# Normalizing both heads of an attention pair with one read over two PSUM banks

## The chip, the cores and the metric

The kernel runs on one core of a Trainium2 chip. The metric is device time of one execution in microseconds: 550.02 us in the median of three runs (549.77 to 550.32). The page and the trace come from one profiled execution.

## The reference, cut to what matters

```python
# attention: 2 batches, 12 heads, 448 positions, head dimension 64
scores = matmul(q, k.T) / 8
scores = where(triu, -1e9, scores); scores -= max(scores)
attn = exp(scores); attn /= sum(attn) + 1e-9
x = (attn @ v), heads side by side            # 896 tokens x 768
# first feed-forward part (768 -> 1536 -> 768)
xn = x / sqrt(mean(x*x) + 1e-6) * rms_g
x = (silu(xn @ w_gate) * (xn @ w_val)) @ w_out
# second part (768 -> 1024 -> 1024 -> 768)
x = ((x @ w1) * (x @ w2)) @ w3 @ w_out2
```

All inputs and the output are float32.

## The kernel before

**Number format.** A float32 operand is split into a float16 high part and a bfloat16 remainder (`halve`: `hi_part`, L442 to L444, and `lo_part`, L447 and L448). A product is three matmuls of such parts (L486). Weights arrive as 64-bit patterns that `fetch` (L459 to L468) turns into float32 by shifts and masks.

**Stages.** (1) Attention, in 12 pairs of heads (two batches, six pairs each). (2) Beside it, `w_prime` multiplies w3 by the last output weight, in 2 x 8 groups of 8 steps of three 384-column matmuls, on bank 3; this is work that TensorE does while attention waits. (3) `norm`, after each batch: the mean square, its power -0.5 (on GpSimd), and a matmul with the diagonal of it. (4) The gate and value stage, 12 units. Each is a product of 2 x 2 blocks in seven products instead of eight (`wino`), with sums of weight quarters (`sums`, on L482 on VectorE or L483 on GpSimd) and seven joins from PSUM (L818), 84 joins in all. (5) The output projection of the first part, (6) eight units of the second part, made as in (4), and (7) three units with the product of w3 and the output weight. From (4) on, a matmul has 448 columns.

**A pair** (`pair`): scores of both heads go to banks 0 to 2, VectorE adds the mask and takes the maximum (L556), ScalarE takes exponentials (L560). The probabilities have to be turned for the product with v. Pairs 0 to 2 turn them on TensorE (`turn`); pairs 3 to 11 split them and have a transfer turn them (`send`, L608), three a pair, queued on SyncE: two with 768 probabilities (rows of 12x128), one with 512 (8x128). The split buffers `hA` (two) and `hB` (one) are free again when the transfer has landed. Then P V: each head has four accumulation groups in its own bank, 4 or 5 (`OB`), 64 columns of output and one that holds the row sum. Three VectorE instructions a head end it: sum x 64 plus an epsilon (L657), reciprocal (L659), product into `x4` (L661). For `norm`, ScalarE sums squares of `x4` (L669).

**What sets the order.** Every instruction is given to a planner (`Plan.add`) with an engine, a cost, what it reads and writes, and a priority: a due time from the pair's or unit's number (`TP`, `GVS`, `OS`, `AS`, `FS`) and an offset by kind (`PO`). Some kinds name other engines, too (`alt`): high parts may go to VectorE or GpSimd, low parts and sums to GpSimd; `BIAS` and `THETA` say how long such work waits for its own engine. `Plan.order` plays the program forward and backward and writes each engine's list. Each engine then runs its list in that order, and waits on semaphores.

Of the kernel before, what the change touches and what calls it, by code (L numbers as in the profile page):

```python
# [8 lines left out]
F32 = mybir.dt.float32  # L9
# [6 lines left out]
ALU = mybir.AluOpType  # L16
PSUM = bass.MemoryType.PSUM

P = 128
B, H, S, D = 2, 12, 448, 64  # L20
# [6 lines left out]
NT = 4  # L27
# [3 lines left out]
GH = 2  # L31
# [4 lines left out]
SV = 2.0**6  # L36
# [1 line left out]

TP = 28.0521
WP0 = -244.6493
WPS = 48.9793
GVS = 6.4864
OS = 3.1806
AS = 4.3573
FS = -5.7914
PO = dict(dq=86.1608, dv=18.1427, vh=-4.1615, vl=31.153, sc=-23.1187, s3=-45.5392, hA=-61.1976, hl=15.902,
    hB=-24.2123, pv=19.2543, sq=-20.7221, nm=29.1952, wm=26.8125, ww=-36.4818, wx=25.6973, g=24.6307,
    a=-40.6597, o=14.4327, f=-41.7402, gm=-30.163, e=10.5623, ae=-45.2952, y=-25.9701, t1=23.8236,  # L50
    mx=19.799, dw=-6.0874)


PASSES = 8
BIAS = {"dve": 17.4016, "pool": 80.0945, "act": 139.3857}
THETA = 0.4843

DA, DB = range(3,12), range(3,12)
# [3 lines left out]
SSB, OB, GB, PB, TB = (0, 1, 2), (4, 5), (3,), (6, 7), (4, 5, 7)  # L62
# [184 lines left out]
def dve_us(n):  # L247
    return n / 960.0 + 0.07
# [26 lines left out]
def fused_kernel(ctx: ExitStack, tc, qk, v, g, wgv, wo, wab, w3t, wout, out):  # L275
    nc = tc.nc
    pl = Plan()
    add = pl.add

    const = ctx.enter_context(tc.tile_pool(name="const", bufs=1))  # L280
    psum = ctx.enter_context(tc.tile_pool(name="psum", bufs=1, space=PSUM))
    bank = [psum.tile([P, 512], F32, name=f"bank{i}") for i in range(8)]


    arena = const.tile([P, ARENA // 2], F16, name="arena")
# [58 lines left out]
    sq = [view(("sq", b), [NT, NG], F32) for b in range(B)]  # L344
    ms = [view(("ms", b), [NT], F32) for b in range(B)]
    rstd = [view(("rstd", b), [NT, 1], F32) for b in range(B)]
    mx_r = Ring("att", "mx", 3, [P, 8], F32)
    rs_r = Ring("att", "rs", 2, [P, NT, 1], F32)
    ri_r = Ring("att", "ri", 2, [P, NT, 1], F32)

    wo2 = [view(("wb", j), [NI, 384], F16 if j == 0 else BF16) for j in range(2)]
    w3 = [view(("w3", it), [2, DF2], F16) for it in range(NI)]
# [176 lines left out]
    def pair(b, gi):  # L529
        p = b * NG + gi  # L530
        x4, kx4 = x4s[:, p % 7], ("x4", p % 7)
        heads[gi] = (x4, kx4)
        t0 = p * TP
        qs, kqs = qs_r.next()
        vs, kvs = vs_r.next()
        vh, kvh = vh_r.next()
        vl, kvl = vl_r.next()
        add("sp", dma_us(P * 2 * S * 4), lambda: nc.sync.dma_start(out=qs, in_=qk[b, gi]), w=[kqs],
            prio=t0 + PO["dq"])
        add("sp", dma_us(P * 512 * 4), lambda: nc.sync.dma_start(out=vs, in_=v[b, gi]), w=[kvs],  # L540
            prio=t0 + PO["dv"])
# [8 lines left out]
        mx, kmx = mx_r.next()  # L550
# [22 lines left out]
        for i in range(3):  # L573
            w = WID[i]
# [38 lines left out]
        blk = tA.rearrange("p h c n -> p (h c) n")  # L613
        for j in range(GH if p in DA else 0):
            send(768, *hA_r.next(), pA[j][0], [pA[j][1] + (i,) for i in range(3)], blk[:, j * 12:j * 12 + 12],
                 [ktA + (c, j) for c in range(3)], 1.8, t0 + PO["hA"])
        for c in range(0, 0 if p in DA else 12, 4):
            turn([pA[j][0][:, OFF[i] + kb * P:OFF[i] + kb * P + P] for i, j, kb in order[c:c + 4]],
                 [tA[:, h, c:c + 4] for h in range(2)],
                 ktA + (c // 4,), [pA[j][1] + (i,) for i, j, _ in order[c:c + 4]], t0 + PO["hA"])  # L620
        if p in DB:
            send(512, *hB_r.next(), pB, [kpB], tB.rearrange("p h c n -> p (h c) n")[:, :, 0:P],
                 [ktB + (h,) for h in range(2)], 1.4, t0 + PO["hB"])
        else:
            turn([pB[:, kb * P:kb * P + P] for kb in range(4)], [tB[:, h, :, 0:P] for h in range(2)], ktB, [kpB], t0 + PO["hB"])

        for j in range(GH):
            ob, ko = o_b.next()
            o = ob[:, :NT * (D + 1)].rearrange("p (t c) -> p t c", t=NT)
            pr = t0 + PO["pv"] + j  # L630

            def pv(i, o=o, j=j):
                n = 3 * (i + 1)
                k = 0
                for kb in range(i + 1):
                    if i < 3:
                        c = where[i, j, kb]
                        if p in DA:
                            c = j * 12 + OFF[i] // P + kb
                        lh, ll = blk[:, c], blk[:, c + (6 if p in DA else 12)].bitcast(BF16)  # L640
                    else:
                        sl = slice(j * D, j * D + P)
                        lh, ll = tB[:, 0, kb, sl], tB[:, 1, kb, sl].bitcast(BF16)
                    r = kb * GH + j
                    for lt, rt, c in ((lh, vh[:, r], D + 1), (lh, vl[:, r], D), (ll, vh[:, r], D + 1)):
                        mm(o[:, i, :c], lt, rt, start=(k == 0), stop=(k == n - 1))
                        k += 1
            for i in range(NT):
                kt = {ktA + (where[i, j, kb] // 4,) for kb in range(i + 1)} if i < 3 else [ktB]
                kt = [k + (h,) for k in sorted(kt) for h in range(2)]  # L650
                if i < 3 and p in DA:
                    kt = [ktA + (c, j) for c in range(3)]
                add("pe", 3 * (i + 1) * 0.0286, lambda pv=pv, i=i: pv(i), r=[
                    *kt, kvh, kvl], w=[ko], prio=pr)
            rs, krs = rs_r.next()
            ri, kri = ri_r.next()
            add("dve", 0.09, lambda o=o, rs=rs: nc.vector.tensor_scalar(  # L657
                rs, o[:, :, D:D + 1], SV, 1.0e-9 * SV, op0=ALU.mult, op1=ALU.add), r=[ko], w=[krs], prio=pr)
            add("dve", 0.1, lambda rs=rs, ri=ri: nc.vector.reciprocal(ri, rs), r=[krs], w=[kri], prio=pr)  # L659
            c = j * D  # L660
            add("dve", dve_us(256), lambda o=o, ri=ri, c=c: nc.vector.tensor_tensor(  # L661
                x4[:, :, c:c + D], o[:, :, 0:D], ri.to_broadcast([P, NT, D]), op=ALU.mult),
                r=[ko, kri], w=[kx4 + (j,)], prio=pr)


        g0, m, q = SQ[b].get(gi, (0, 0, 0))
# [287 lines left out]
```

## Time and profile before

| | |
|---|---|
| median of three runs | 550.02 us |
| profiled execution, its span | 548.47 us, 546.7 us |
| TensorE busy | 524.3 us (96%) |
| VectorE busy | 495.8 us (91%) |
| ScalarE, GpSimd busy | 338.8 us (62%), 237.5 us (43%) |
| chain that ended last | TensorE 54%, VectorE 23%, transfers 8%, issue 5%, ScalarE 3% |

PE is TensorE's matmul row, PEld its weight loads, DVE VectorE, ACT ScalarE, POOL GpSimd and SP SyncE, which only issues transfers. Matmuls overlap, so a busy PE also holds time in which a matmul waits for its data; how many were done in a stretch says more. [...]

### The profile page before, as it was taken

The page shows a single profiled execution, that of the slowest core. Times are in us where ns is not written, and L with a number is a line of the kernel's source. Part 1 is how long each engine was busy: PE and PEld are TensorE (multiplying, and loading weights), DVE is VectorE, ACT ScalarE, POOL GpSimd, SP SyncE. Part 2 cuts the span into 40 slices and gives each one's busy share as a digit, 9 for nine tenths or more (in the row PEclk, how much of TensorE's full clock was granted, in tenths as well). Part 3 has the DMA queues.
Part 4 walks back from the last instruction along what each step waited for, and adds up shares of the span by engine and source line. Part 5 has one row for each costly group of instructions (what it writes and reads, how often), then busy time and mean ns, then how long its engine had stood idle before and what let it go on. Part 6 is the DMA issues. An engine that isn't in the chain of part 4 may idle for free.

```text
span 546.7 us, 9215 instructions
## 1 busy us (share of the span) xinstructions
PE 524.3 (96%) x3442; PEld 286.6 (52%) x3442; DVE 495.8 (91%) x909; ACT 338.8 (62%) x492; POOL 237.5 (43%) x198
## 2 busy tenths in 40 slices
PE   6899999999899999999999999999999999999997
PEld 4565565564666554444555455555555555454553
DVE  6999999989959999999999999899658999999953
ACT  5988887896678676557464767676336553633210
POOL 4534364676453837053656420140211846673400
PEclk9999999999999999999999999999999999999999
DMA  8888799999951133334242446517104211000021
GB/s 276 288 278 263 222 252 218 258 248 184 279 112 59 34 127 130 122 109 173 70 162 78 158 172 252 208 59 236 52 0 168 65 59 59 0 1 0 35 101 68
DMA packets 55197, 77.02 MB, mean 141 GB/s; under 512 B 39792, under 2 KB 41328, under 8 KB 55152
## 3 DMA queue, kind: packets, MB, share of 16 engines
q1 hardware_dynamic: 55152, 76.43, 48.1%
q8 instruction: 27, 0.44, 0.3%
q14 instruction: 18, 0.15, 0.1%
HBM read 64.23 MB, written 2.75 MB: 123 GB/s over the span
## 4 chain that ended last, share of the span: by engine, by line
PE 54%; DVE 23%; DMA 8%; issue 5%; ACT 3%; POOL 0%; DVEq 0%; SPq 0%; ACTq 0%
PE bank L486 54%; DVE arena L818 6%; DVE arena L447 6%; DMA arena<-arena 5%; DVE cv L468 3%; DVE st L482 3%; DVE cv L461 2%; DVE arena L482 2%; DMA st<-in_wout 2%; ACT st L464 1%; DMA st<-in_w3t 1%; DVE arena L556 1%; ACT arena L442 1%; ACT arena L560 1%; DVE arena L547 0%
## 5 line engine op out<-in xcount | busy, mean ns | idle before, releaser
L486 PE MATMUL bank<-arena 128*128 128x448 f16 (+10 forms) x2976 | 446.1, 315 | 14.7 <-ACT wpr L516 3.9
L486 PEld LDWEIGHTS <-arena 128*128 128x128 f16 x3048 | 248.8, 98 | 229.0 <-issue 22.1
L464 ACT ACTIVATE st<-st 128x768 uint16<-128x768 uint16 (+2 forms) x72 | 117.6, 1658 | 32.6 <-DVE cv L461 29.9
L818 DVE TENSOR_TENSOR arena<-bank,arena 128x448 f32<-128x448 f32 x161 | 92.1, 612 | 18.1 <-PE bank L486 17.8
L442 ACT ACTIVATE arena<-arena 128x448 f16<-128x448 f32 (+2 forms) x90 | 53.9, 612 | 40.4 <-DVE arena L482 27.8
L468 DVE SCALAR_TENSOR_TENSOR cv<-st,cv 128x768 int32<-128x768 int32 (+2 forms) x84 | 75.1, 903 | 2.8 <-ACT st L464 2.6
L448 POOL TENSOR_TENSOR arena<-arena 128x448 bf16<-128x448 f32 (+2 forms) x29 | 49.6, 1713 | 56.7 <-ACT arena L442 44.5
L486 PE MATMUL bank<-xs,arena 128*128 128x448 f16 x360 | 72.4, 353 | 1.7 <-ACT arena L815 1.1
L447 DVE TENSOR_TENSOR arena<-arena 128x448 bf16<-128x448 f32 (+2 forms) x80 | 61.2, 780 | 2.4 <-ACT arena L442 1.1
L442 ACT ACTIVATE arena<-cv 128x768 f16<-128x768 f32 (+2 forms) x61 | 41.0, 679 | 32.5 <-DVE cv L468 18.6
L461 DVE TENSOR_SCALAR cv<-st 128x768 int32<-128x768 int32 (+2 forms) x84 | 50.0, 600 | 7.3 <-DMA st<-in_wout 4.2
L448 POOL TENSOR_TENSOR arena<-cv,arena 128x384 bf16<-128x384 f32 (+2 forms) x31 | 44.4, 1434 | 24.8 <-ACT arena L442 24.2
L483 POOL TENSOR_TENSOR arena<-arena 128x448 f32<-128x448 f32 x23 | 30.1, 1314 | 35.6 <-DVE arena L818 21.3
L560 ACT ACTIVATE arena<-arena 128x384 f32<-128x384 f32 (+3 forms) x84 | 41.2, 518 | 5.8 <-DVE arena L556 5.2
L444 POOL TENSOR_SCALAR arena<-cv 128x384 f16<-128x384 f32 (+2 forms) x22 | 20.2, 918 | 55.7 <-DVE cv L468 31.1
L447 DVE TENSOR_TENSOR arena<-cv,arena 128x768 bf16<-128x768 f32 (+2 forms) x53 | 43.3, 824 | 0.8 <-POOL arena L444 0.7
L447 DVE TENSOR_TENSOR arena<-st,arena 128x1536 bf16<-128x1536 f32 (+1 forms) x25 | 42.1, 1682 | 0.1
L482 DVE TENSOR_TENSOR arena<-arena 128x448 f32<-128x448 f32 x57 | 37.5, 668 | 4.1 <-ACT arena L864 4.1
L442 ACT ACTIVATE arena<-st 128x1536 f16<-128x1536 f32 (+1 forms) x22 | 30.5, 1389 | 17.4 <-DVE st L482 7.7
L556 DVE CUSTOM_DVE_ANT_0 arena<-bank,arena 128x384 f32<-128x384 f32 (+3 forms) x84 | 35.7, 441 | 1.9 <-PE bank L486 1.2
L486 PEld LDWEIGHTS bank<-arena 64*128 64x128 f32 (+2 forms) x288 | 27.5, 178 | 19.0 <-issue 5.2
L815 ACT ACTIVATE arena<-bank 128x448 f32<-128x448 f32 x23 | 12.6, 546 | 25.3 <-PE bank L486 15.2
(69 smaller groups left out, 310.2 us busy)
## 6 DMA issues: line engine op xcount, KB each, us to landing
st<-in_wgv SPq DMA_DIRECT2D x24, 768.0 KB, 4.5
st<-in_wab SPq DMA_DIRECT2D x16, 768.0 KB, 4.4
st<-in_wo SPq DMA_DIRECT2D x12, 768.0 KB, 4.4
st<-in_w3t SPq DMA_DIRECT2D x16, 512.0 KB, 4.8
st<-in_wout SPq DMA_DIRECT2D x16, 384.0 KB, 3.9
arena<-in_qk SPq DMA_DIRECT2D x12, 448.0 KB, 5.1
arena<-in_v SPq DMA_DIRECT2D x12, 256.0 KB, 3.8
out_t<-arena SPq DMA_DIRECT2D x12, 224.0 KB, 1.9
```

Source lines behind the costliest of these rows:

```text
L442: add("act", act_us(n), lambda: nc.scalar.activation(hi, src, AF.Copy), r=r, w=w, prio=prio, alt=(("dve", dve2_us(n), lambda: nc.vector.te ...
L447: add("dve", dve_us(n), lambda: nc.vector.tensor_tensor(lo, src, hi, op=ALU.subtract), r=r, w=w, prio=prio, port=True, alt=(("pool", pool_ ...
L448: port=True, alt=(("pool", pool_us(n), lambda: nc.gpsimd.tensor_tensor(lo, src, hi, op=ALU.subtract)),))
L461: add("dve", dve2_us(n), lambda: nc.vector.tensor_scalar(cv, hi, 3, 0x3FFFFFFF, op0=ALU.logical_shift_left, op1=ALU.bitwise_and), r=[ks], ...
L464: add("act", ACT_TOP * n - 0.08, lambda: nc.scalar.activation(b[:, :, 2], b[:, :, 1], AF.Copy, scale=1.0 / 8192, bias=-8191.0 / 16384), w= ...
L468: add("dve", dve_us(n), lambda: nc.vector.scalar_tensor_tensor(cv, hi, -0x3FFFFFF9, cv, op0=ALU.bitwise_and, op1=ALU.bitwise_or), r=[ks], ...
L482: add("dve", dve_us(n), lambda: nc.vector.tensor_tensor(out, a, b, op=op), port=True, alt=(("pool", pool_us(n) + 0.1, lambda: nc.gpsimd.te ...
L483: ("pool", pool_us(n) + 0.1, lambda: nc.gpsimd.tensor_tensor(out, a, b, op=op)),), **kw)
L486: nc.tensor.matmul(*a, **k)
L556: add("dve", dve_us(w), lambda: nc.vector.tensor_tensor_reduce(out=sc[:, :w], in0=ss[:, :w], in1=m, scale=-CSC, scalar=3.0e38, op0=ALU.add ...
L560: add("act", act_us(w) + 0.1, lambda: nc.scalar.activation(dst, sc[:, :w], AF.Exp, bias=mx[:, c:c + 1], scale=-1.0), r=[ksc, kmx + (c,)], ...
L818: add("dve", dve_us(S), lambda: nc.vector.tensor_tensor(dst, ps, y, op=ALU.add), r=[kp, ky], w=[kd], prio=p)
```

## The change

`o_b` still hands out banks 4 and 5, head 0 and head 1, but both are now views of one PSUM tile of two banks. The three normalizing instructions move out of the loop over heads: one set per pair reads both banks, and it waits for both heads' products. The planner's cost of a turning transfer goes from 1.8 to 1.9 and from 1.4 to 1.8. All due times, offsets and the three `BIAS` values have new numbers, of which two lines are shown.

```diff
-PO = dict(dq=86.1608, dv=18.1427, vh=-4.1615, vl=31.153, sc=-23.1187, s3=-45.5392, hA=-61.1976, hl=15.902,
...
+PO = dict(dq=77.7592, dv=-40.5165, vh=-6.106, vl=33.6109, sc=-35.4643, s3=-35.7215, hA=-116.2841,
...
-BIAS = {"dve": 17.4016, "pool": 80.0945, "act": 139.3857}
+BIAS = {"dve": 23.0593, "pool": 108.7578, "act": 107.956}
...
-    bank = [psum.tile([P, 512], F32, name=f"bank{i}") for i in range(8)]
+    two = psum.tile([P, GH, 512], F32, name="banks45")
+    bank = [two[:, i - 4] if i in OB else psum.tile([P, 512], F32, name=f"bank{i}") for i in range(8)]
...
-                 [ktA + (c, j) for c in range(3)], 1.8, t0 + PO["hA"])
+                 [ktA + (c, j) for c in range(3)], 1.9, t0 + PO["hA"])
...
-                 [ktB + (h,) for h in range(2)], 1.4, t0 + PO["hB"])
+                 [ktB + (h,) for h in range(2)], 1.8, t0 + PO["hB"])
...
-            rs, krs = rs_r.next()
-            ri, kri = ri_r.next()
-            add("dve", 0.09, lambda o=o, rs=rs: nc.vector.tensor_scalar(
-                rs, o[:, :, D:D + 1], SV, 1.0e-9 * SV, op0=ALU.mult, op1=ALU.add), r=[ko], w=[krs], prio=pr)
-            add("dve", 0.1, lambda rs=rs, ri=ri: nc.vector.reciprocal(ri, rs), r=[krs], w=[kri], prio=pr)
-            c = j * D
-            add("dve", dve_us(256), lambda o=o, ri=ri, c=c: nc.vector.tensor_tensor(
-                x4[:, :, c:c + D], o[:, :, 0:D], ri.to_broadcast([P, NT, D]), op=ALU.mult),
-                r=[ko, kri], w=[kx4 + (j,)], prio=pr)
+        o = two[:, :, :NT * (D + 1)].rearrange("p j (t c) -> p j t c", t=NT)
+        kos = [("bank", i) for i in OB]
+        rs, krs = rs_r.next()
+        ri, kri = ri_r.next()
+        pr = t0 + PO["pv"] + 1
+        four = lambda t: t.rearrange("p (j t) c -> p j t c", j=GH)
+        add("dve", 0.09, lambda: nc.vector.tensor_scalar(
+            four(rs), o[:, :, :, D:D + 1], SV, 1.0e-9 * SV, op0=ALU.mult, op1=ALU.add), r=kos, w=[krs], prio=pr)
+        add("dve", 0.1, lambda: nc.vector.reciprocal(ri, rs), r=[krs], w=[kri], prio=pr)
+        add("dve", dve_us(512), lambda: nc.vector.tensor_tensor(
+            x4.rearrange("p t (j c) -> p j t c", j=GH), o[:, :, :, 0:D], four(ri).to_broadcast([P, GH, NT, D]),
+            op=ALU.mult), r=[*kos, kri], w=[kx4 + (j,) for j in range(GH)], prio=pr)
```

Line numbers of the changed kernel are one higher from L283 on and four higher behind the normalization (L657, L659, L661 become L662, L664, L665).

VectorE's list where the last pair is normalized, before (`cv` and `st` are buffers in which gate weights are unpacked; banks 65 and 66 are banks 4 and 5):

```order
L468 SCALAR_TENSOR_TENSOR cv_78<-st_74,cv_78 128x768
L657 TENSOR_SCALAR arena<-bank_65 128x4
L468 SCALAR_TENSOR_TENSOR cv_77<-st_73,cv_77 128x768
L657 TENSOR_SCALAR arena<-bank_66 128x4
L659 RECIPROCAL arena<-arena 128x4 x2
L661 TENSOR_TENSOR arena<-bank_65,arena 128x4x64
L661 TENSOR_TENSOR arena<-bank_66,arena 128x4x64
L676 TENSOR_REDUCE arena<-arena 128x4
```

The same place in VectorE's list now, from the normalization of the last pair but one on:

```order
L662 TENSOR_SCALAR arena<-banks_61 128x8
L548 SCALAR_TENSOR_TENSOR arena<-arena 128x512
L664 RECIPROCAL arena<-arena 128x8
L462 TENSOR_SCALAR cv_77<-st_73 128x768
L665 TENSOR_TENSOR arena<-banks_61,arena 128x2x4x64
L469 SCALAR_TENSOR_TENSOR cv_77<-st_73,cv_77 128x768
L662 TENSOR_SCALAR arena<-banks_61 128x8
L664 RECIPROCAL arena<-arena 128x8
L665 TENSOR_TENSOR arena<-banks_61,arena 128x2x4x64
L462 TENSOR_SCALAR cv_76<-st_72 128x768
L467 TENSOR_SCALAR st_72<-st_72 128x768
```

Six instructions of the pair became three over both banks, and unpacking moved behind them, ahead of the mean square.

SyncE's list at the last turning transfers, before (the three of the last pair are the last three):

```order
L608 DMA_TRANSPOSE arena<-arena 128x12x128
L540 DMA arena<-in_v 128x512
L459 DMA st_72<-in_wgv 128x1536
L608 DMA_TRANSPOSE arena<-arena 128x12x128
L459 DMA st_73<-in_wgv 128x1536
L608 DMA_TRANSPOSE arena<-arena 128x8x128
L608 DMA_TRANSPOSE arena<-arena 128x12x128
```

The same place in SyncE's list now:

```order
L609 DMA_TRANSPOSE arena<-arena 128x12x128
L541 DMA arena<-in_v 128x512
L609 DMA_TRANSPOSE arena<-arena 128x12x128
L609 DMA_TRANSPOSE arena<-arena 128x8x128
L609 DMA_TRANSPOSE arena<-arena 128x12x128
L460 DMA st_72<-in_wgv 128x1536
L460 DMA st_71<-in_wgv 128x1536
```

Two loads of gate weights (`wgv`) moved behind the last turn.

GpSimd's list at its end, before (`wpr` is the product of `w_prime`; its quarters' sums have 256 elements):

```order
L483 TENSOR_TENSOR st_72<-wpr,st_72 128x256
L483 TENSOR_TENSOR st_73<-wpr 128x256
L483 TENSOR_TENSOR st_72<-wpr 128x256
L483 TENSOR_TENSOR st_71<-st_71,wpr 128x256
L448 TENSOR_TENSOR arena<-wpr,arena 128x768
L483 TENSOR_TENSOR st_72<-wpr 128x256
L483 TENSOR_TENSOR st_71<-wpr,st_71 128x256
L483 TENSOR_TENSOR st_72<-wpr,st_72 128x256
```

GpSimd's list at its end now:

```order
L484 TENSOR_TENSOR st_72<-wpr 128x256
L484 TENSOR_TENSOR arena<-arena 128x448
L449 TENSOR_TENSOR arena<-st_71,arena 128x1024
L445 TENSOR_SCALAR arena<-st_70 128x1024
L449 TENSOR_TENSOR arena<-wpr,arena 128x768
```

Most of these sums went to VectorE's list.

## Rows read from the trace of the kernel before

**Rows 1.** Stretches by stage: length, then busy time (instructions) of each engine, clock, transfers.

```profile
0.00:70.00 70.00, 61.75 (x469) 37.88 (x470) 62.06 (x164) 56.92 (x87) 29.70 (x43) 1.00 0.83 268
70.00:100.00 30.00, 28.39 (x343) 16.29 (x342) 28.45 (x93) 25.03 (x55) 18.11 (x20) 1.00 1.12 238
100.00:153.50 53.50, 49.78 (x553) 31.45 (x552) 49.42 (x128) 41.71 (x79) 32.53 (x27) 1.00 1.12 232
153.50:168.70 15.20, 14.59 (x139) 11.38 (x140) 9.21 (x18) 11.59 (x27) 5.63 (x6) 1.00 0.29 76
168.70:310.50 141.80, 137.97 (x725) 70.23 (x724) 140.37 (x201) 90.82 (x113) 74.02 (x52) 1.00 0.32 109
310.50:404.00 93.50, 93.50 (x495) 48.37 (x496) 82.40 (x124) 57.82 (x69) 19.25 (x12) 1.00 0.45 156
404.00:505.60 101.60, 100.91 (x533) 51.88 (x532) 98.71 (x145) 48.56 (x60) 52.17 (x34) 1.00 0.14 47
505.60:546.70 41.10, 37.38 (x197) 19.12 (x196) 25.20 (x42) 6.37 (x8) 6.12 (x5) 1.00 0.18 68
```

**Rows 2.** The chain that ended last, pieces in order: start, length, what.

```profile
146.64 6.85 DMA arena<-arena
153.53 5.37 PE bank L486 x66
...
310.48 151.33 PE bank L486 x799
```

**Rows 3.** Groups by form, VectorE: busy us, mean ns, idle time ahead and its releasers.

```profile
L447 DVE TENSOR_TENSOR arena<-arena 128x448 bf16<-128x448 f32 x60 | 39.7, 680 | 0.5 <-POOL arena L444 0.5
L482 DVE TENSOR_TENSOR arena<-arena 128x448 f32<-128x448 f32 x57 | 37.5, 668 | 4.1 <-ACT arena L864 4.1
L447 DVE TENSOR_TENSOR arena<-st,arena 128x1536 bf16<-128x1536 f32 x19 | 34.8, 1831 | 0.1
...
L661 DVE TENSOR_TENSOR arena<-bank,arena 128x256 f32<-128x256 f32 x24 | 9.5, 411 | 0.0
...
L482 DVE TENSOR_TENSOR st<-cv 128x384 f32<-128x384 f32 x13 | 8.5, 656 | 0.0
...
L466 DVE TENSOR_SCALAR st<-st 128x768 uint16<-128x768 uint16 x8 | 8.5, 1061 | 0.0
...
L601 DVE TENSOR_TENSOR arena<-bank,arena 128x512 bf16<-128x512 f32 x12 | 8.1, 678 | 0.1
...
L482 DVE TENSOR_TENSOR st<-wpr 128x256 f32<-128x256 f32 x7 | 4.1, 588 | 0.0
...
L659 DVE RECIPROCAL arena<-arena 128x4 f32<-128x4 f32 x24 | 3.9, 168 | 0.0
...
L657 DVE TENSOR_SCALAR arena<-bank 128x4 f32<-128x4 f32 x24 | 3.5, 151 | 1.2 <-PE bank L486 1.2
```

**Rows 4.** VectorE in order of time, normalizing instructions back to back: start, us, instruction.

```profile
129.02 0.15 DVE L657 TENSOR_SCALAR arena<-bank 128x4 f32<-128x4 f32 x1
129.09 0.41 DVE L661 TENSOR_TENSOR arena<-bank,arena 128x256 f32<-128x256 f32 x1
129.42 0.16 DVE L659 RECIPROCAL arena<-arena 128x4 f32<-128x4 f32 x1
129.50 0.59 DVE L556 CUSTOM_DVE_ANT_0 arena<-bank,arena 128x448 f32<-128x448 f32 x1
```

**Rows 5.** Line L482 alone: shortest, median and longest in ns, first and last start.

```profile
L482 DVE TENSOR_TENSOR arena<-arena x57: 606/611/1550, 166.7 to 504.4; 128x448 f32<-128x448 f32 x57
```

**Rows 6.** SyncE's queue in order of time, the last pair's turning transfers.

```profile
141.70 0.38 SPq L459 DMA_DIRECT2D st<-in_wgv  x1
142.27 2.72 SPq L608 DMA_TRANSPOSE arena<-arena  x1
146.21 0.33 SPq L459 DMA_DIRECT2D st<-in_wgv  x1
146.64 6.20 SPq L608 DMA_TRANSPOSE arena<-arena  x2
```

**Rows 7.** Who waited for whom: TensorE for the normalizing product, us in total, times, longest.

```profile
PE bank L486 <- DVE arena L661: 1.4, 2, 1.2
```

More of the change, by code (lines that the diff above doesn't have):

```diff
@@ L37 @@
 CSC = 1.0 / 8.0
[L41 to L47, printed above, removed]
-PO = dict(dq=86.1608, dv=18.1427, vh=-4.1615, vl=31.153, sc=-23.1187, s3=-45.5392, hA=-61.1976, hl=15.902,
-    hB=-24.2123, pv=19.2543, sq=-20.7221, nm=29.1952, wm=26.8125, ww=-36.4818, wx=25.6973, g=24.6307,
-    a=-40.6597, o=14.4327, f=-41.7402, gm=-30.163, e=10.5623, ae=-45.2952, y=-25.9701, t1=23.8236,
-    mx=19.799, dw=-6.0874)
+TP = 27.8378
+WP0 = -245.8258
+WPS = 50.5471
+GVS = 6.7175
+OS = 3.5723
+AS = 4.4797
+FS = -8.2001
+PO = dict(dq=77.7592, dv=-40.5165, vh=-6.106, vl=33.6109, sc=-35.4643, s3=-35.7215, hA=-116.2841,
+    hl=22.6624, hB=-33.9427, pv=24.7154, sq=-60.5725, nm=29.7288, wm=27.3571, ww=-34.6109, wx=54.8086,
+    g=20.3381, a=-40.8814, o=-2.6777, f=-32.9588, gm=-31.3816, e=28.8562, ae=-39.8349, y=-19.4493,
+    t1=22.8432, mx=18.7762, dw=-21.4831)
 PASSES = 8
-BIAS = {"dve": 17.4016, "pool": 80.0945, "act": 139.3857}
+BIAS = {"dve": 23.0593, "pool": 108.7578, "act": 107.956}
 THETA = 0.4843
@@ L347, in fused_kernel @@
     mx_r = Ring("att", "mx", 3, [P, 8], F32)
-    rs_r = Ring("att", "rs", 2, [P, NT, 1], F32)
-    ri_r = Ring("att", "ri", 2, [P, NT, 1], F32)
+    rs_r = Ring("att", "rs", 2, [P, GH * NT, 1], F32)
+    ri_r = Ring("att", "ri", 2, [P, GH * NT, 1], F32)
     wo2 = [view(("wb", j), [NI, 384], F16 if j == 0 else BF16) for j in range(2)]
```

## Prediction

> **What bounds the kernel now.** I read the table of stages first, then the chain of waits, then VectorE's rows, and the issue queue last. The stages [rows 1] fall into two kinds. From 168.7 us on (the four feed-forward stages) TensorE does little but multiply: the longest unbroken stretch of the chain holds 799 matmuls in 151.33 us, 0.1894 us each [rows 2]. At that rate the 725 matmuls of 168.7 to 310.5 need 137.3 of 141.8 us, so 4.5 us are waits; the 495 of 310.5 to 404 and the 533 of 404 to 505.6 need 93.8 and 100.9 us, so waits there are under 1 us. All that can be won after 168.7 us is then some 5 us. VectorE is busy for 140.37 of 141.8 us in the first of these stages: the 4.5 us are waits for VectorE. In 404 to 505.6 it is busy for 98.71 of 101.6 us and only just keeps up.
>
> Before 168.7 us TensorE is not the bound. VectorE is busy for 62.06 of the first 70 us, with the transfers at a share of 0.83, then for 28.45 of 30 and 49.42 of 53.5 us. In 153.5 to 168.7 it is busy for only 9.21 of 15.2 us, since it waits for the last pair of heads. The chain there runs through the turning transfers: one of 6.85 us on it lands at 153.49, and the last P V products start on it [rows 2]. So the end of the attention is set by the last pair's splits on VectorE, its turning transfers, and then the normalization this change edits.
>
> **The change part by part.** The sums are made against the profiled execution, 548.47 us (span 546.7 and 1.77 around it); the median of the runs is 550.02, 1.55 above it, and I add that at the end.
>
> *Normalization.* Per head there are three VectorE instructions: 0.151, 0.168 and 0.411 us long [rows 3]. On a busy VectorE they cost less than they last, because the next one starts before the one ahead has ended: 129.02 to 129.09, 129.09 to 129.42, 129.42 to 129.50 [rows 4], so 0.07, 0.33 and 0.08, with rounding 0.49 per head and 0.98 per pair. Now there are three per pair. The two short ones keep their price, 0.15 together; the product grows from 256 to 512 elements, and the nearest pair of rows that read PSUM puts 256 more elements at 0.678 - 0.411 = 0.267 us [rows 3], so 0.60. A pair costs 0.75, a saving of 0.23, and 12 pairs save 2.8 us. If the two-bank read cost nothing extra per element it would be 0.50 per pair, 5.8 us; if it took twice the 256-element product and its own start, nothing is saved beyond the short pair, 1.8 us. I take 2.8.
>
> [...] The spacing of the rows [rows 4] shows that most of the short instructions' length is covered here.
>
> *Work that changes engine.* The planner picks an engine for each split and each sum of the weights. Of the 104 sums of weight quarters, 61 stood on VectorE and 82 do now. I count VectorE's rows up to the last of the 84 joins of the gate and value stage, apart from the normalization: 12 more sums of 384 (0.656), 4 fewer products or sums of 448 (0.668), 4 fewer low parts of 448 (0.680) and 2 fewer of 1536 (1.831) [rows 3]: +7.9 - 2.7 - 2.7 - 3.7 = -1.2. The single rows left over are some 14, near zero. With the normalization VectorE has 4.0 us less to do by then. Where it falls: about 2 us before the last split of the last pair (10 of the 12 normalizations, the rest cancels), about 2 between there and the first join, none inside the stage.
>
> Behind that join VectorE has 8 more sums of 256 (0.588), 5 more low parts of 448, 3 more products of 448, 3 fewer shifts of 768 (1.061), and small ones worth -1.8: +4.7 + 3.4 + 2.0 - 3.2 - 1.8 = +5.1 us. GpSimd is relieved of the same work. That gives some back: a sum of 448 on VectorE takes 0.606 at the least, 0.611 in the median, and up to 1.550 [rows 5], and its mean in the table is 0.668 [rows 3], a tenth more than undisturbed. Less GpSimd work means fewer such stretched rows.
>
> *Turning transfers.* Their number and size stay. In the queue the load of gate weights between the last pair's turns (146.21 [rows 6]) now stands behind them, and of seven such loads ahead of the last turn five are left. These loads share the transfer engines, whose share is 1.12 from 70 to 153.5 us [rows 1]. I price this at nothing, with up to 3 us below as its bound: two loads less in a stretch of 53.5 us whose last hop is 6.85 us.
>
> *The sum.* Attention: VectorE is busy for 93% of 70 to 153.5 us, so most of its 2.0 us comes through: -1.7 (bounds 0, if the turns alone set the pace, and -4.6 with the transfers relieved as well). The hand-over and gate stage: -1.8 of the 2.0 us, for VectorE has hardly an idle microsecond there and TensorE has 4.5 us of waits to give back (bounds 0 and -4.0). Behind 404 us: 5.1 us more in a stretch where VectorE has 2.9 idle, less what GpSimd's relief gives back: +1.0 (bounds 0 and +4). Together -2.5: 546.0 for a profiled execution, **547.5** as a median.
>
> **The rivals.**
> *The shared banks become a wait (slower).* Before, head 0's bank was free as soon as that head was normalized; now both wait for head 1's products, and the next pair's first product waits for the joint instruction. TensorE takes its list in order, so scores, w' steps and products behind it stand too. Today two such waits cost 1.4 us [rows 7]. There are 11 hand-overs. From the last product of a pair, the joint work needs 0.75 us plus what stands between its three rows, mostly two score reductions, some 2 us in all; in TensorE's list the tightest hand-over (pair 9 to 10) has one score pair and four w' steps ahead, 12 matmuls at about 0.16 (an estimate, 0.1894 x 384/448), 1.9 us plus the scores. It decides if VectorE stands more than a microsecond behind at most hand-overs: then 11 x 0.7 = 8 us, half of it hidden where the turns are late anyway, +4, less the 2 that the gate stage gains: 552. Against it: the planner knows the dependency and spread the products out, and VectorE's list is shorter. [...]
> *The turns set the end anyway (no change).* The last hop of 6.85 us [rows 2] does not care for 2 us of VectorE, which then idles longer than today's 6 us before 168.7; the gate stage's gain pays for the end: 549.5.
> *The end pays it all back.* VectorE's 5.1 us behind the gate stage come through by 3 to 4 where it is already at 98.71 of 101.6: 550 to 551.
> *The transfers are relieved too (faster still).* The attention ends 4.6 earlier: 544.5.
>
> **How the numbers follow.** What a measurement tells from no change is about 0.2%, 1.1 us. The forecast has 0.45 (0.39 of it faster, 0.06 within), faster still 0.16, turns set the end 0.16 (all within), paid back 0.10 (half within, half slower), shared banks 0.13 (slower). Faster 0.55, within 0.27, slower 0.18. The range leaves out the last tenth on either side: 543.5 to 552.
>
> **What would show it.** Right: the first 448-column product starts 1 to 4 us before 168.7; the three joint rows are spaced by 0.75 in all, the product lasts near 0.68; VectorE's wait for P V products stays near 1.2 us [rows 3] and TensorE's for the joint product at or below 1.4 us; the 4.5 us of waits up to the end of the gate stage shrink by about 2; VectorE is busier than 98.71 in the second unit stage. Wrong: the first product starts later than 168.7, TensorE's waits for the joint product are above 4 us, or the waits behind 404 us grow by more than 2 us.

## The result, and the profile after

The changed kernel takes 557.81 us in the median of four runs (556.89 to 558.93), against 550.14 for the kernel before beside it: a ratio of 1.0141, 95% interval 1.0118 to 1.0164. The forecast was 547.5 with a range of 543.5 to 552. It was wrong in size and in sign. The profiled execution has a span of 555.1 us.

The stretches of [rows 1], of the changed kernel:

```profile
0.00:70.00 70.00, 62.26 (x477) 38.27 (x477) 61.10 (x151) 54.63 (x85) 38.25 (x52) 0.95 0.79 264
...
153.50:168.70 15.20, 12.06 (x119) 9.31 (x118) 9.21 (x14) 7.64 (x22) 3.98 (x4) 0.89 0.44 159
168.70:310.50 141.80, 135.49 (x724) 70.88 (x723) 137.86 (x195) 89.82 (x114) 80.42 (x51) 1.00 0.31 106
310.50:404.00 93.50, 92.17 (x487) 47.51 (x486) 84.45 (x129) 64.17 (x69) 15.25 (x9) 1.00 0.46 161
404.00:505.60 101.60, 100.85 (x534) 52.05 (x532) 96.41 (x147) 48.75 (x62) 39.71 (x27) 1.00 0.15 47
```

The windows are those of the kernel before; from the gate stage on, the changed kernel is 2.6 us and more behind it in them. The first row has a clock of 0.95 and GpSimd at 38.25 us, where it was 1.00 and 29.70. In 153.5 to 168.7 TensorE is busy for 12.06 us instead of 14.59, at a clock of 0.89. In the gate and value stage VectorE is no longer busy nearly throughout (137.86 for 140.37): it has idle time that it had not before, while GpSimd does more (80.42 for 74.02). In 310.5 to 404, where TensorE had not idled, it now does 487 matmuls for 495.

VectorE's groups by form, which answer to [rows 3]:

```profile
L483 DVE TENSOR_TENSOR arena<-arena 128x448 f32<-128x448 f32 x56 | 34.1, 630 | 4.3 <-ACT arena L704 2.5 <-ACT arena L868 1.3 <-ACT arena L843 0.5
...
L665 DVE TENSOR_TENSOR arena<-banks,arena 128x512 f32<-128x512 f32 x12 | 8.2, 682 | 0.0
...
L664 DVE RECIPROCAL arena<-arena 128x8 f32<-128x8 f32 x12 | 2.3, 194 | 0.1
L662 DVE TENSOR_SCALAR arena<-banks 128x8 f32<-128x8 f32 x12 | 1.9, 156 | 1.9 <-PE banks L487 1.9
```

The joint product takes 0.682 us, next to the 0.68 that was reckoned. From the start of each normalizing row to the next row's start, idle time left out, a pair costs 0.86 us in the mean of the twelve, where the trace before has 1.04: 2.2 us saved in all, and 2.8 were reckoned.

TensorE from 168 us on, in order of time: the waits of over 0.3 us ahead of matmuls that write the two-bank tile (`banks`), with the idle time and its releaser in brackets.

```profile
169.40 2.00 PE L487 MATMUL banks<-arena 128*128 128x128 f32 x16 [0.36 <-ACT arena L704]
...
214.43 1.86 PE L487 MATMUL banks<-arena 128*128 128x448 f16 x9 [0.87 <-DVE arena L822]
...
255.60 1.86 PE L487 MATMUL banks<-arena 128*128 128x448 f16 x9 [0.92 <-DVE arena L822]
...
353.51 3.56 PE L487 MATMUL banks<-arena 128*128 128x448 f16 x18 [0.69 <-ACT arena L868]
...
401.98 3.56 PE L487 MATMUL banks<-arena 128*128 128x448 f16 x18 [0.63 <-ACT arena L868]
...
545.56 0.73 PE L487 MATMUL banks<-arena 128*128 128x448 f16 x3 [0.63 <-ACT arena L819]
```

These are six waits, 4.1 us. In the program's semaphores the reason can be counted: 19 instructions of TensorE on bank 4 or 5 wait for a reader of the other bank, and at least 15 readers on VectorE and ScalarE wait for a product in the other one. In the kernel before there is none of either. The program orders a tile as a whole: banks 4 and 5 serve the mean square and all later products as well, and there they are now one buffer.

The end of the attention, VectorE, GpSimd and TensorE in that order:

```profile
156.00 0.17 DVE L662 TENSOR_SCALAR arena<-banks 128x8 f32<-128x8 f32 x1 [1.32 <-PE banks L487]
156.20 0.20 DVE L664 RECIPROCAL arena<-arena 128x8 f32<-128x8 f32 x1
156.44 0.69 DVE L665 TENSOR_TENSOR arena<-banks,arena 128x512 f32<-128x512 f32 x1
...
159.94 0.17 DVE L683 TENSOR_SCALAR arena<-arena 128x4 f32<-128x4 f32 x1
...
163.25 1.32 DVE L688 TENSOR_TENSOR arena<-arena 128x512 f32<-128x512 f32 x1 [1.87 <-POOL arena L685]
```

```profile
159.97 1.00 POOL L484 TENSOR_TENSOR st<-cv 128x384 f32<-128x384 f32 x1 [14.34 <-DVE arena L680]
161.04 1.19 POOL L484 TENSOR_TENSOR st<-st,cv 128x384 f32<-128x384 f32 x1
162.19 1.02 POOL L685 TENSOR_TENSOR arena<-arena,mhalf 128x4 f32<-128x4 f32 x1
```

```profile
164.62 3.53 PE L487 MATMUL banks<-arena 128*128 128x128 f32 x16 [2.56 <-DVE arena L688]
...
171.24 1.86 PE L487 MATMUL bank<-xs,arena 128*128 128x448 f16 x9
```

The last joint product ends at 157.13. Before, the last two products ended at 157.53:

```profile
156.78 0.75 DVE L661 TENSOR_TENSOR arena<-bank,arena 128x256 f32<-128x256 f32 x2
```

Then the mean square's power (L685) stands behind two sums in GpSimd's list and starts 2.1 us after its input is there. TensorE idles for 2.56 us, and its next 16 matmuls take 3.53 us, at a granted clock of 0.52 (165 to 168 us, below). The first 448-column product starts at 171.24 instead of 168.67.

A table from the traces, one profiled execution each (us), for this kernel and most of the experiments told below. First and last product are the starts of the first and last matmul of 448 columns from the gate stage on.

| kernel | first product | last product | between |
|---|---|---|---|
| before | 168.67 | 542.63 | 373.96 |
| changed | 171.24 | 551.04 | 379.80 |
| before, one tile | 171.91 | 549.17 | 377.26 |
| two tiles | 169.39 | 543.48 | 374.09 |
| banks apart behind | 172.78 | 547.90 | 375.12 |
| changed, filled | 170.07 | 549.86 | 379.79 |
| apart, filled | 172.52 | 547.32 | 374.80 |
| two tiles, filled | 169.76 | 544.52 | 374.76 |
| power first | 167.53 | 543.07 | 375.54 |

The changed kernel loses 5.8 us between the two and 2.6 ahead of the first. A single execution can lie far from its kernel's median: that of the two tiles is the fastest of six (549.32, median 552.51), and that of "apart, filled" is 2.7 us slower than its median.

### The profile page after: what moved, and what is told of

Its sections match the earlier page's. It is cut to its first block, busy times and chain, and to the rows that moved or that the text cites. A ratio compares the mean times of both kernels' runs of the same rounds, so it can differ in the third digit from the quotient of the medians.

```text
span 555.1 us, 9164 instructions
## 1 busy us (share of the span) xinstructions
PE 525.2 (95%) x3434; PEld 288.4 (52%) x3434; DVE 499.4 (90%) x885; ACT 341.4 (61%) x493; POOL 223.6 (40%) x185
## 5 line engine op out<-in xcount | busy, mean ns | idle before, releaser
L487 PE MATMUL bank<-arena 128*128 128x448 f16 (+7 forms) x1802 | 345.4, 359 | 12.8 <-DVE arena L822 5.1
L487 PE MATMUL banks<-arena 128*128 128x65 f16 (+4 forms) x1174 | 114.9, 254 | 8.9 <-DVE arena L688 2.6
L449 POOL TENSOR_TENSOR arena<-cv,arena 128x384 bf16<-128x384 f32 (+2 forms) x36 | 57.6, 1604 | 62.2 <-ACT arena L443 50.2
L822 DVE TENSOR_TENSOR arena<-bank,arena 128x448 f32<-128x448 f32 x127 | 73.8, 612 | 6.9 <-PE bank L487 6.5
L487 PE MATMUL bank<-xs,arena 128*128 128x448 f16 (+1 forms) x252 | 50.8, 352 | 0.0
L449 POOL TENSOR_TENSOR arena<-arena 128x448 bf16<-128x448 f32 (+2 forms) x29 | 40.0, 1388 | 22.2 <-ACT arena L443 17.1
L561 ACT ACTIVATE arena<-arena 128x128 f32<-128x128 f32 (+3 forms) x84 | 41.0, 518 | 9.2 <-DVE arena L557 5.1
L557 DVE CUSTOM_DVE_ANT_0 arena<-bank,arena 128x256 f32<-128x256 f32 (+3 forms) x84 | 35.2, 440 | 4.9 <-ACT arena L561 2.5
L448 DVE TENSOR_TENSOR arena<-cv,arena 128x768 bf16<-128x768 f32 (+2 forms) x48 | 38.0, 799 | 0.0
L822 DVE TENSOR_TENSOR arena<-banks,arena 128x448 f32<-128x448 f32 x34 | 20.4, 613 | 12.2 <-PE banks L487 12.2
```

The costliest lines, as they stand in the source:

```text
L448: add("dve", dve_us(n), lambda: nc.vector.tensor_tensor(lo, src, hi, op=ALU.subtract), r=r, w=w, prio=prio, port=True, alt=(("pool", pool_ ...
L449: port=True, alt=(("pool", pool_us(n), lambda: nc.gpsimd.tensor_tensor(lo, src, hi, op=ALU.subtract)),))
L487: nc.tensor.matmul(*a, **k)
L557: add("dve", dve_us(w), lambda: nc.vector.tensor_tensor_reduce(out=sc[:, :w], in0=ss[:, :w], in1=m, scale=-CSC, scalar=3.0e38, op0=ALU.add ...
L561: add("act", act_us(w) + 0.1, lambda: nc.scalar.activation(dst, sc[:, :w], AF.Exp, bias=mx[:, c:c + 1], scale=-1.0), r=[ksc, kmx + (c,)], ...
L822: add("dve", dve_us(S), lambda: nc.vector.tensor_tensor(dst, ps, y, op=ALU.add), r=[kp, ky], w=[kd], prio=p)
```

## The experiments

**Two separate tiles.** The changed kernel's lists word for word; sums and products read bank by bank, each pair of reads in the joint one's place.

```diff
-    two = psum.tile([P, GH, 512], F32, name="banks45")
-    bank = [two[:, i - 4] if i in OB else psum.tile([P, 512], F32, name=f"bank{i}") for i in range(8)]
+    bank = [psum.tile([P, 512], F32, name=f"bank{i}") for i in range(8)]
```

> The changed kernel with banks 4 and 5 as two PSUM tiles again. The lists of all engines stay word for word; VectorE reads the two banks in two instructions each for the sums and the products (12 x about 0.4 us = 4.8 us more VectorE time, nothing else). Theory A (a tile of two banks is tracked as one, so that a product in bank 4 waits for the reader of bank 5 and the other way round): the waits of TensorE behind its first 448-column product, 11.5 us in the changed kernel and 6.5 before, fall to 7 or less; time 551.5 to 554. Theory B (the refitted numbers give worse lists): nothing changes there, and VectorE's extra work comes on top: 557.5 to 561.

Measured: 552.51 us (549.32 to 556.74, six runs), ratio 1.0085 [1.0048, 1.0123], in theory A's range. The six waits listed above are gone, and the length between first and last product is that of before.

**The kernel before with the joint tile alone.** The opposite edit: six instructions a pair as before, lists word for word.

```diff
-    bank = [psum.tile([P, 512], F32, name=f"bank{i}") for i in range(8)]
+    two = psum.tile([P, GH, 512], F32, name="banks45")
+    bank = [two[:, i - 4] if i in OB else psum.tile([P, 512], F32, name=f"bank{i}") for i in range(8)]
```

> The kernel before with banks 4 and 5 as one PSUM tile of two banks and nothing else: same lists, normalization still per head. Theory A: waits between the two banks, in the attention (the products of head 1 wait while head 0 is normalized) and in every later stage: 554 to 564. Theory B: no change, 549 to 551.

Measured: 556.55 us (555.04 to 558.75), 1.0148 [1.0113, 1.0182], in theory A's range. Declaring the two banks as one tile, with nothing else changed, costs as much as the whole change. TensorE's waits ahead of `banks` include these:

```profile
347.38 3.57 PE L487 MATMUL banks<-arena 128*128 128x448 f16 x18 [0.63 <-ACT arena L865]
483.87 3.56 PE L487 MATMUL banks<-arena 128*128 128x448 f16 x18 [1.37 <-DVE arena L819]
543.68 0.73 PE L487 MATMUL banks<-arena 128*128 128x448 f16 x3 [0.63 <-ACT arena L816]
```

Here the hand-overs inside the attention cost something, too. The first product comes 3.2 us later than before, and TensorE's waits for normalizing instructions (in total, times, longest) come to 2.7 us where it waited 1.4 before [rows 7]:

```profile
PE banks L487 <- DVE arena L662: 2.0, 4, 0.8
PE banks L487 <- DVE arena L658: 0.7, 3, 0.3
```

In this kernel one head's products wait while the other head is normalized; in the changed kernel both are normalized at once.

**The two halves of the change, planned anew.** The numbers and turning costs without the joint normalization, then the joint normalization with the old numbers and costs.

> The kernel before with the changed kernel's numbers (due times, offsets, biases, cost of a turning transfer), normalization per head, two tiles. Theory A: most of the loss is gone, 549 to 553. Theory B: the numbers carry the loss, 555 to 559.

> The changed kernel with the numbers of the kernel before: joint read over one tile of two banks, old due times, offsets, biases and transfer costs. Theory A: 554 to 559, with the waits behind the first 448-column product at 10 us or more. Theory B: 548 to 551.

Measured: 572.24 us, 1.0424 [1.0382, 1.0466], and 569.79 us, 1.0387 [1.0361, 1.0413]. Both missed every theory. Two more kernels took the turning costs alone: the kernel before with the new ones, the changed kernel with the old ones.

> The kernel before, with nothing changed but the two turning costs (1.8 to 1.9 and 1.4 to 1.8), so the lists are planned anew with the old numbers. If the numbers are fitted to one set of lists and any other input gives lists that nobody has selected, 555 to 575, like the two halves of the change (572 and 570). If the half's slowness came from the normalization's form alone, 548 to 552.

> The changed kernel with the two turning costs as before, the new numbers and the joint normalization kept. If the numbers are fitted to one set of lists, 562 to 575; if the turning costs matter little to the lists, 556 to 560.

Measured, two runs each: 562.22 us, 1.0224 [1.0189, 1.0260], and 569.43 us, 1.0356 [1.0322, 1.0390]. In all four, most of the loss lies between first and last product: 388 to 403 us in their profiled executions, instead of 374. In the first and the last of the four, TensorE also has its longest waits around the end of the attention, of 3.2, 5.2 and 10.1 us (total, times, longest):

```profile
PE bank L486 <- ACT wpr L516: 9.6, 7, 3.2
PE bank L486 <- DVE arena L684: 5.6, 2, 5.2
```

```profile
PE banks L487 <- DVE arena L688: 11.0, 2, 10.1
```

The planner's numbers fit the lists they were chosen for. All four other inputs gave lists 2 to 4% slower, so the price of one half can't be had by leaving the other out. The experiments below keep the planned lists, but for the instructions that they add or replace and for one place in the order of two of them.

**Banks apart behind the attention.** The joint normalization stays; when the last pair is normalized, the two-bank tile is given back and two separate ones take its place.

```diff
+    def apart():
+        early.__exit__(None, None, None)
+        pool = ctx.enter_context(tc.tile_pool(name="apart", bufs=1, space=PSUM))
+        for i in OB:
+            late[i] = pool.tile([P, 512], F32, name=f"bank{i}")
...
+            if p == B * NG - 1:
+                apart()
```

> The changed kernel's lists word for word and its joint normalization, but banks 4 and 5 are one tile only until the last pair is normalized, and two separate tiles from there on. Theory A (the time is lost where a product or join on one of the two banks waits for the other bank's reader, in the mean square's matmuls and the feed-forward stages): 551.5 to 553.5, as with two separate tiles throughout (552.5); TensorE's waits for the joins of L822 fall from 6.9 us to 3 or 4. Rival B (the pair's hand-over inside the attention carries it): 556 to 558, no change from the changed kernel. Rival C (the granted clock carries it): 556 to 558 too, with the clock still at 0.985 to 0.993.

Measured: 553.52 us (550.03 to 555.12, eleven runs), 1.0067 [1.0041, 1.0094]: by the ratios 0.74%, some 4.1 us, less than the changed kernel. TensorE's waits for the joins fall from 6.9 to 4.0 us. So these 4 us are not lost in the hand-overs inside the attention, which still go through one tile.

**The gaps filled.** `filler` issues two matmuls on zeros: 13 times ahead of the third turn on TensorE, 10 times ahead of the last mean square's first matmul.

```diff
+                for _ in range(13 if turns[0] == 3 else 0):
+                    filler()
...
+                for _ in range(10 if first else 0):
+                    filler()
```

> The changed kernel with 26 matmuls on zeros of 252 columns ahead of the third turn on TensorE (16.4 to 19.7 us, where it idles 3.3 us) and 20 ahead of the first matmul of the last mean square (162 to 164.6 us, where it idles 2.6 us), all else alike. The two stretches behind these gaps ran at 0.64 and 0.51 (20 to 28 us) and at 0.52 (165 to 168 us). Theory C (the lost clock carries the time): 551 to 553, mean clock 0.997 or more. Theory A: the clock rises to 0.997, but attention is not bound by TensorE before 160 us, and only the 1.5 us at 165 to 168 come back: 555.5 to 557.

> Both edits: banks apart behind the attention, and the two gaps filled. If A and C act side by side, the gains add up: 552.5 for the first less 1.5 to 2 for the second, 550.5 to 551. If the clock carries most, 547 to 549. If B holds, 555 or more.

> Two separate tiles throughout (sums and products read bank by bank, five VectorE instructions a pair in the joint ones' places) and the two gaps filled. Against the kernel with the banks apart behind the attention and the gaps filled, this one has 24 more VectorE instructions of 0.07 to 0.33 us spacing, 2 to 3 us in all. If VectorE's time in the attention comes through, as the prediction held, it is 1.5 to 2.5 us slower than that one; if not, the same within 1 us. Its own time by A and C: 550.5 to 552; against two tiles without filling (552.5) the filling is worth 1 to 3 us.

Measured: 555.81 us (553.74 to 556.93), 1.0119 [1.0084, 1.0154]; with the banks apart 550.50 (547.59 to 554.28, twelve runs), 1.0017 [0.9989, 1.0044]; with two tiles 550.33 (548.44 to 551.76, twelve runs), 1.0015 [0.9995, 1.0036]. Stretches around the two gaps, the changed kernel and then the same filled; the third number from the end is the granted clock:

```profile
16.00:20.00 4.00, 0.70 (x7) 0.33 (x4) 4.00 (x9) 3.12 (x6) 2.18 (x3) 1.00 0.90 312
20.00:24.00 4.00, 4.00 (x34) 2.76 (x34) 3.64 (x10) 3.27 (x6) 2.85 (x3) 0.64 0.86 259
24.00:28.00 4.00, 4.00 (x50) 3.04 (x48) 3.70 (x10) 4.00 (x7) 2.19 (x4) 0.51 0.84 304
162.00:165.00 3.00, 0.44 (x3) 0.38 (x2) 1.75 (x3) 2.27 (x3) 2.03 (x3) 0.91 0.00 0
165.00:168.00 3.00, 3.00 (x17) 3.00 (x16) 1.37 (x3) 0.00 (x0) 0.00 (x0) 0.52 0.00 0
```

```profile
20.00:24.00 4.00, 3.75 (x42) 2.68 (x41) 4.00 (x12) 4.00 (x7) 2.04 (x3) 1.00 0.80 256
24.00:28.00 4.00, 3.99 (x57) 2.49 (x58) 2.86 (x9) 3.22 (x6) 3.02 (x4) 1.00 0.91 309
162.00:165.00 3.00, 2.57 (x24) 1.99 (x22) 1.39 (x2) 2.27 (x3) 2.39 (x3) 1.00 0.00 0
165.00:168.00 3.00, 2.88 (x24) 2.74 (x24) 2.05 (x4) 0.98 (x2) 0.00 (x0) 1.00 0.02 5
```

Behind a stretch with TensorE busy for 0.70 of 4 us the clock is 0.64 and then 0.51, and from 28 to 32 us it is 1.00 again; behind one with 0.44 of 3 us it is 0.52. With the gaps filled it is 1.00 from 20 to 28 us and from 162 to 168. Over the runs, the mean clock is 0.990 for the changed kernel and 0.996 filled. By the ratios, the filling is worth 0.22% (1.2 us) by itself, and there the intervals overlap, 0.50% (2.7 us) with the banks apart and 0.70% (3.8 us) with two tiles. In the changed kernel that is what theory A expected and not theory C: the first product comes 1.2 us earlier, and the length behind it stays at 379.8. The last two kernels differ by 0.2 us: reading both banks at once, 36 instructions instead of 60, brings nothing that can be measured here. What it saves and what its hand-overs through one tile may cost inside the attention are not told apart.

**The power first.** In the kernel with two tiles filled, the two sums ahead of the power on GpSimd move behind it (and 16 of the 20 matmuls on zeros at that place go).

```diff
+    at = next(k for k, f in enumerate(issue) if f is power[1])
+    held = [k for k, f in enumerate(issue[:at]) if any(f is q for q in pool_sums)][-2:]
+    issue = [f for k, f in enumerate(issue[:at + 1]) if k not in held] + [issue[k] for k in held] + issue[at + 1:]
```

> Two separate tiles and the filled start, as in the kernel with two tiles filled (550.3), and on GpSimd the power of the last mean square moved ahead of two sums of 384 that stand before it in the changed kernel's list (with only 4 matmuls on zeros left ahead of the mean square's first matmul). In that kernel the power starts 2.1 us after VectorE has its input, because the two sums run first (160.58 to 162.82). Theory T (the end of the attention is a chain: last turn, normalization, squares, power, diagonal, matmuls): the first 448-column product starts 1.5 to 2.2 us earlier, 548.2 to 549. Rival (VectorE's splits behind the matmuls are late anyway, so the chain has slack): within 0.5 us of 550.3.

Measured: 549.38 us (547.91 to 551.33, twelve runs) beside 550.00 for the kernel before, 0.9987 [0.9969, 1.0005]. That lies between the ranges of the two theories. The power now starts at 160.18, 0.1 us after its input, and the first product at 167.53, 2.2 us earlier than in the kernel with two tiles filled; 0.6 us of these stood ahead of the power already, since the last normalizing product ends at 157.30 instead of 157.90:

```profile
160.18 1.26 POOL L699 TENSOR_TENSOR arena<-arena,mhalf 128x4 f32<-128x4 f32 x1 [14.73 <-DVE arena L697]
```

```profile
167.53 1.86 PE L492 MATMUL bank<-xs,arena 128*128 128x448 f16 x9
```

Of the 2.2 us some 1.5 are left in the time (0.28% by the two ratios, whose intervals overlap): the chain is there in the trace, as expected, and part is given back in the gate and value stage (134.3 us, and 133.4 with two tiles filled, from the first product to the end of the 725th matmul of 448 columns, counted here and in the last experiment from the program's start with the attention's own). This is the best of the kernels that compute everything, and it can't be told from the kernel before.

**Products made twice.** The kernel before, each normalizing product issued a second time.

```diff
+            def twice(o=o, ri=ri, c=c):
+                for _ in range(2):
+                    nc.vector.tensor_tensor(x4[:, :, c:c + D], o[:, :, 0:D], ri.to_broadcast([P, NT, D]), op=ALU.mult)
+            add("dve", dve_us(256), twice, r=[ko, kri], w=[kx4 + (j,)], prio=pr)
```

> The kernel before, lists word for word, with each of the 24 normalizing products on VectorE made twice, the second over the first. That is 24 x 0.33 = 7.9 us more for VectorE, all but 0.7 of it ahead of the last pair's end. The prediction's step (VectorE is busy for 93% of 70 to 153.5 us, so most of what it is relieved of, or loaded with, comes through): +5 to +7, 554.5 to 557. Theory T (the turning transfers and hand-overs pace the pairs, VectorE's small work lies in its waits): +0 to +2.5, 549.5 to 552.

Measured: 555.91 us (554.40 to 557.53), 1.0111 [1.0090, 1.0132], +5.9.

VectorE's group of these products, and two of them in order of time:

```profile
L664 DVE TENSOR_TENSOR arena<-bank,arena 128x256 f32<-128x256 f32 x48 | 19.7, 418 | 0.8
```

```profile
155.45 0.87 DVE L664 TENSOR_TENSOR arena<-bank,arena 128x256 f32<-128x256 f32 x2
156.24 0.15 DVE L657 TENSOR_SCALAR arena<-bank 128x4 f32<-128x4 f32 x1
```

The second product does not overlap the first (0.87 us for two of 0.42): 10.2 us more on VectorE (9.5 in [rows 3]), where 7.9 were expected. The first product of the gate stage comes at 176.44, 7.8 us later. So load on VectorE in the attention does come through, 5.9 of the 10.2 us by the runs, as the prediction held and theory T did not.

**Low parts left out in the gate stage.** The kernel with the power first, where GpSimd's low parts of the gate and value weights become a write of zeros: part of the weights' remainder is left out. There are fourteen such rows in the stage (eight of 384, four of 768, two of 1536; 33.5 us in all), not seven as the expectation counted.

```diff
+        on_pool = lambda: nc.gpsimd.tensor_tensor(lo, src, hi, op=ALU.subtract)
+        if gate[0]:
+            on_pool = lambda: nc.gpsimd.memset(lo, 0.0)
```

> The kernel with the power first, lists word for word, with seven of GpSimd's low parts in the gate and value stage (two of 768 at 3.15 us, one of 1536 at 3.1, four of 384 at 1.8, some 16.6 us in all) replaced by a write of zeros: this leaves out a part of the weights' remainder. VectorE's list is untouched. From the first to the 725th 448-column product the kernel with the power first took 134.3 us and the kernel before 131.9, with VectorE busy for 132.5 and 130.5. Theory G (GpSimd's longer hold beside VectorE stretches VectorE's rows, which set the pace of this stage): the joins of shifted weights at L470 fall from 1.21 us to below 1.10 in that stage and the stage shrinks by 1.5 to 3 us; 546.5 to 548. Rival (the stage waits for weights on ScalarE or for transfers): the stage within 0.5 us, 549 to 549.8.

Measured: 547.15 us (545.55 to 550.09, ten runs) beside 550.42, 0.9957 [0.9929, 0.9985], 0.30% less than with the power first, where the intervals overlap. From the first product to the 725th such matmul it takes 132.0 us instead of 134.3 in the traces, as theory G expected. The joins of shifted weights on VectorE between 167 and 301 us, with the power first and then with the low parts out:

```profile
L470 DVE SCALAR_TENSOR_TENSOR cv<-st,cv 128x768 int32<-128x768 int32 x18 | 21.7, 1211 | 1.7 <-ACT st L466 1.7
```

```profile
L475 DVE SCALAR_TENSOR_TENSOR cv<-st,cv 128x768 int32<-128x768 int32 x18 | 19.1, 1063 | 0.2 <-ACT st L471 0.2
```

VectorE's list is the same, and these rows are shorter where GpSimd's low parts write zeros and read nothing: 1.06 us for 1.21 in the mean. So are the 28 sums of 384 in the same stretch, which also have two inputs: 18.9 us in place of 23.3. In neither trace does TensorE or VectorE wait for a row of GpSimd there, so that the low parts come earlier is not what shortens the stage. That VectorE's rows last longer beside GpSimd's shows in the trace of the kernel before, too: of the 57 sums of 448 on VectorE [rows 5], the 41 with no GpSimd row beside them last 0.613 us in the mean, and the 14 with one beside them for more than half of their length 0.829. The shift ahead of the joins, with one input, went the other way (0.73 to 0.90 us a row); why was not shown.

## Why the prediction was wrong, step by step

**The failed step: what the joint tile costs outside the normalization.** The part on the normalization priced its three instructions and left banks 4 and 5 otherwise as they were. The rival on shared banks put the price in the eleven hand-overs of the attention, at +4 for the attention and a chance of 0.13. The place was wrong: TensorE's matmuls wait nowhere for the joint product (before, 1.4 us for L661 in [rows 7]), VectorE waits 1.9 us for P V products instead of 1.2. The price stands in the stages where each bank had its own user. By the ratios it is 0.74%, some 4 us, by taking the tile apart behind the attention, and 0.56%, some 3 us, by two tiles. Alone in the kernel before, where the heads are still normalized one by one, the tile costs 7.7 us; in its trace 3.2 us of the loss come ahead of the first product and 3.3 behind the 1220th matmul of 448 columns, so there the rival's place was right in part. The diff showed the one tile, and the code who else takes banks 4 and 5; the prediction did not ask it.

**Not considered: the clock.** The forecast took [rows 1] with its clock of 1.00 for granted. The new lists leave TensorE idle for 3.3 us at 16.7 us and for 2.56 at 162, and the lower clock behind the two (down to 0.51 and 0.52) costs some 1 to 4 us together, by the filled kernels (0.22, 0.50 and 0.70%).

**Attention, -1.7: came out as +2.6 to the first product.** That VectorE's time comes through was right for more load (the doubled product). For less load it was not: its last normalization ends only 0.4 us earlier. Part of the relief was not there: weight shifts of 384 last 0.61 us a piece up to 157 us where they lasted 0.40 (16 of them, 3.4 us), while the joins behind them got shorter (0.56 for 0.63). GpSimd works 8.6 us more in the first 70 us; that this stretches the shifts was not shown. What else stood in the way was not isolated; the turning transfers, which the rival "turns set the end" named, are the candidate. Behind the normalization the order of unpacking and sums, which the prediction did not price, cost some 2 us up to the first product: the power behind two sums. With the gaps filled and the power first, the first product starts at 167.53, 1.1 us earlier than before, in one execution.

**Gate and value stage, -1.8: came out as +2.5.** The prediction's 725 matmuls, counted from the first product on, take 144.9 us instead of 142.4. (Counted as in the last experiment it is +3.9, since the kernel before takes two of its waits between the two counts.) With two tiles they take 141.8, so the tile makes the loss, and at most 0.5 us of the forecast gain is left; with two tiles filled it is 142.5. The step that failed there is "less GpSimd work means fewer such stretched rows". GpSimd is relieved over the whole kernel (237.5 to 223.6 us), but in this stage it does 6.4 us more; the joins of shifted weights there last 1.21 us for 1.08, and the last experiment shows that GpSimd's low parts stretch them (1.21 with these, 1.06 without). A sum over the kernel was used for one stage.

**Behind 404 us, +1.0:** 148.7 for 147.0 us from the 1220th matmul of 448 columns of the program to the last, and 147.7 with two tiles filled: right, and 1.0 of the 1.7 is the tile's. In the fixed window of 404 to 505.6 us VectorE looks less busy (96.41 for 98.71), but over the same matmuls it is busier, as forecast: 129.95 us for 126.68.

**Right:** the normalization's rows and the joint product's length, with 2.2 us saved for 2.8. The whole durations of a pair's rows add up to 1.46 us before and 1.03 now, but by the rows' starts a pair costs 1.04 and 0.86. The saving brought nothing that can be measured (550.50 with the joint read, 550.33 without it, both filled); why, while doubled products cost 5.9 us, stays open.

By the ratios, taken in this order, the 1.41% is: the tile 0.74, the gaps 0.50, the power 0.28 (two tiles filled against the same with the power first), and -0.11 left for all that was forecast, which is within the interval of no change. Each part is a difference of two ratios that are known to 0.2 or 0.3, and in another order they would differ: the gaps alone, filled first, are 0.22.

## What to carry to other kernels

Before two buffers are joined for one reader, list every other user of either: a joint tile is ordered as one, and the price stands where the buffers had separate lives. Here the new lists of the other engines left TensorE idle for 3.3 and 2.56 us, with a clock of 0.51 and 0.52 behind these gaps: read the granted clock behind each new gap. Experiments on a planned kernel keep the lists word for word, since the fitted planner answered every edit here with slower lists.

## What the runs showed of the hardware

With the products made twice, the second of a pair, over the same output, started later behind the first than a product over another output did: pairs last 0.87 us (at 155.45, 159.86 and 161.18 us), of products of 0.42, so the second starts 0.45 us after the first, while two products over different outputs in a row last 0.75 (156.78 us in the kernel before), a start after 0.34.

The program with two tiles spread from 549.3 to 556.7 us over six runs at mean clocks of 0.994 to 0.980; with the gaps filled it spread from 548.4 to 551.8. Behind the wait for the first input, before 10 us, TensorE had been idle for 3.2 us in the changed kernel's profile, and the clock stayed at 1.00 up to 20 us. With the banks apart it had been idle for 1.8 us there, and the clock fell (0.80 from 8 to 12 us, 0.78 from 12 to 16). So the length of a gap alone does not tell what it costs in one execution.
